# Token-order q reads and held output stores in a sliding-window attention + adapter-mixture kernel

## The chip, the cores and the metric

The kernel runs on one core of a Trainium2 chip. The metric is the device time of one execution, in microseconds. The engines are named as in the profile: PE (TensorE, with PEld for its weight loads), DVE (VectorE), ACT (ScalarE), POOL (GpSimd) and SP (SyncE, which here only issues DMAs; SPq is its queue).

## The reference, cut to what matters

Eight batches of eight heads, 576 tokens, head width 64. Each token attends to the tokens at most 32 away; the output of attention, with heads side by side (512 wide), goes through a mixture of eight rank-16 adapters of which the best two are used.

```
q, k, v: (8, 8, 576, 64) fp32
scores = q @ k^T / 8 ; scores = -1e9 where |i - j| > 32
attn   = softmax(scores) ; x = attn @ v            -> x: (4608, 512)
logits = x @ w_gate (512 x 8) ; top 2, softmax over the two -> w
out    = x + sum over the two e of w_e * (x @ A[e] (512 x 16)) @ B[e] (16 x 512)
```

## The kernel before

**Order.** A planner written in Python (`Planner.run`, L108) simulates the engines with estimated durations and due times and so fixes, before compilation, in which order each engine gets its instructions. `P.add(name, engine, duration, due, ...)` registers a task; `deps` are what it waits for, `soft` are dependences of order alone, `take` and `drop` reserve and free buffers of a pool. `LEAN` (L31) shifts the due time of each kind of task. On the chip each engine then runs its list strictly in order and waits on semaphores[...].

**Loads.** q and k come as tiles of 128 rows; a row holds 16 consecutive tokens of one head pair, so that `raw` is [128, 2, 16*64] in fp16 (POOL-issued DMA, `load`, L390). v comes in half batches through SP (`load_v`, L400) into one of 5 `vraw` buffers, and POOL casts it into `vbd` (`cast_v`, L451). The pool `ring` limits the v loads in flight. A batch has two v pairs (e = 0, 1) of two loads (h = 0, 1): 32 v loads in all.

**Scores.** PE transposes `raw` (L474), ACT moves k to `kT` in token order (L499) and DVE moves q to `qT`, [128, 16, 1156], where token 16 i + r lies at `qT[:, r, i]` (L497). A score tile (`score`, L539) covers four key blocks of 64 tokens for two head pairs: four matmuls put the mask into PSUM (L544), sixteen add k.q for 64 keys and 128 queries (L556). Its q operand is read as h, r, s (half, token within 16, group of 16), so the 128 query columns are in a permuted order, with four neighbouring elements at a time:

```
rhs=qT[p0:p0 + 64, :, c0:c0 + 8].rearrange("p r (h s) -> p h r s", h=2),
```

ACT takes exp into `PT` (L564). There are 36 score tiles.

**Attention output.** PE multiplies `PT` with `vbd` (`pv`, L595, and `pv_group` for the last batch, L624), DVE divides by the sum (`norm`, L613) into `xs`, rows in the permuted order.

**Adapters.** For each batch: transpose x (L700), DVE copies it (L705), logits and x @ A in one product (`zl`, L718), ACT copies (L731), gating on DVE (L740 to L761), transpose of the weighted z (L768), and its eviction by ACT (`moe_ez`, L771), which turns the columns to token order on the way. Then `moe_pd` (L782) adds z @ B and x; x is multiplied with `po_`, a permutation matrix made from the identity by POOL (L341), so that its rows come out in token order too. ACT moves the result to one of four `ob` tiles (L795), three blocks j for each batch, and SP stores it (`moe_st`, L797: L806 for single row groups, L801 for pairs), four store DMAs for each batch.

**Fillers.** `fill` (L319) places matmuls of a zero tile (L326) early in the kernel. `ldw` and `cw` load and cast the adapter weights through `Af`, `Gf` and `Bf`.

Of the kernel before, what the change touches and what calls it, by code (L numbers as in the profile page):

```python
# [23 lines left out]
class Planner:  # L24
# [5 lines left out]
    STICK = 0.3  # L30
    LEAN = {"cv": -0.54, "cvb": 46.78, "cw": -20.23, "cz": -10.49, "ek": 141.88,  # L31
            "eo": 48.48, "eoz": -5.02, "eq": -29.69, "ex": 32.88, "exx": -143.53,
            "exxz": -6.85, "ez": -111.14, "ezz": -35.61, "g1": 8.51, "g1z": 14.29,
            "g2": -11.82, "g2z": 45.73, "g3": 8.11, "g3z": -4.63, "ge": -13.97,
            "gez": -0.93, "ident": 11.01, "ld": -3.77, "ldw": 2.33, "lv": 89.29,
            "mask": -43.21, "nm": 2.69, "nmg": 12.33, "pad": 12.33, "pd": 138.17,
            "pdz": -1.64, "perm": 26.94, "pv": -35.98, "pvg": 4.54, "sc": 44.71,
            "st": -31.48, "stz": -8.25, "tr": -7.71, "wm": -4.16, "xT": -4.3, "xTz": -5.83,
            "zT": 88.34, "zTz": 6.27, "zero": 5.31, "zl": 45.91}
    SWITCH = 0.095  # L40
# [175 lines left out]
def kernel(  # L216
# [44 lines left out]

    NRAW, NKB, NVR, NVB, NPT, NX, NOB, NW = 3, 3, 5, 6, 6, 4, 4, 4
    HV = NP * NB // 2
# [18 lines left out]
    ident = const.tile([128, 128], F16, name="ident")  # L282
    po_ = const.tile([128, 128], F16, name="po_")
    mask = const.tile([128, 2, RR, 4], F16, name="mask")
    WA_sb = const.tile([128, NP, ER + E], F16, name="WA")
    B_sb = const.tile([128, DD], F16, name="Bsb")
    Af = const.tile([128, E, 4, R], F32, name="Af")
    Gf = const.tile([128, 4, E], F32, name="Gf")
    Bf = const.tile([128, DD], F32, name="Bf")

# [11 lines left out]
    P.pool("rc", 3)  # L302
    P.pool("ring", 3)
    place = {}
# [10 lines left out]

    zero = const.tile([128, DD], F16, name="zero")
    warm = []
# [22 lines left out]

    def c_perm():  # L341
        nc.gpsimd.tensor_copy(
            out=po_.rearrange("p (h s r) -> p h s r", h=2, s=4),
            in_=ident.rearrange("p (h r s) -> p h s r", h=2, s=4))

    def c_mask():
        nc.gpsimd.memset(mask, 0.0)
        for h in range(2):
            blk = mask[64 * h:64 * h + 64]
            nc.gpsimd.affine_select(out=blk, in_=blk, compare_op=ALU.is_ge, fill=NEG,  # L350
                                    base=0, channel_multiplier=-1,
                                    pattern=[[64, 2], [1, RR], [16, 4]])
            nc.gpsimd.affine_select(out=blk, in_=blk, compare_op=ALU.is_ge, fill=NEG,
                                    base=64, channel_multiplier=1,
                                    pattern=[[-64, 2], [-1, RR], [-16, 4]])

# [23 lines left out]
    P.add("ident", "POOL", 0.6, -19.9, c_ident, ["ld0.0.0"])  # L380
    P.add("perm", "POOL", 0.3, 0, c_perm, ["ident"])
    P.add("mask", "POOL", 2.3, -15, c_mask, ["ld0.0.1"])
# [17 lines left out]
    def load_v(b, e, h):  # L400
# [4 lines left out]
                          in_=src[:, HV * e:HV * e + HV])  # L405

    def load_w():
        nc.sync.dma_start(out=Af.rearrange("p e j r -> p e (j r)"),
                          in_=moe_A.rearrange("e (p j) r -> p e (j r)", j=4))
        nc.sync.dma_start(out=Gf.rearrange("p j e -> p (j e)"),  # L410
                          in_=moe_w_gate.rearrange("(p j) e -> p (j e)", j=4))
        nc.sync.dma_start(out=Bf, in_=moe_B.rearrange("e r d -> (e r) d"))

    def cast_w():
        nc.vector.tensor_copy(
            out=WA_sb[:, :, 0:ER].rearrange("p j (e r) -> p j e r", r=R),
            in_=Af.rearrange("p e j r -> p j e r"))
        nc.vector.tensor_copy(out=WA_sb[:, :, ER:], in_=Gf)
        nc.vector.tensor_copy(out=B_sb, in_=Bf)

    prev = []
    for t in range(NTI):
        hs = ((0, 64), (64, 128)) if t in SPLIT else ((0, 128),)
        for x, (lo, hi) in enumerate(hs):
            for w in (1, 0):
                due = tile_due(t) - 6 + 0.1 * (1 - w) if t else -20
                whole = lo == 0 and hi == 128 and 128 * t % BI + 128 > BI
                gate = GATE.get(t, []) if w == 1 and x == 0 else []
                P.add(f"ld{t}.{w}.{x}", "POOL", 1.2 if whole else 0.62, due + 0.3 * x,
                      lambda t=t, w=w, lo=lo, hi=hi: load(t, w, lo, hi),  # L430
                      prev + gate, lat=1.3,
                      take=[] if x else [("raw" + "qk"[w], t)])
                P.add(f"dq{t}.{w}.{x}", "Q0", 2.8 * (hi - lo) / 128, 0, None,
                      [f"ld{t}.{w}.{x}"], lat=0.8, pkt=172.0)
                prev = [f"ld{t}.{w}.{x}"]
    prev = ["pace"] if PACE else []
    for b in range(B):
        for e in range(2):
            for h in range(2):
# [5 lines left out]
                      pkt=18.0, drop=[("ring", (b, e, h))])  # L445
    P.add("ldw", "SP", 2.0, -2, load_w, WDEP, lat=1.2, take=[("ring", "w")])
    P.add("dw", "Q1", 1.8, -10, None, ["ldw"], lat=0.8, pkt=18.0, drop=[("ring", "w")])
    P.add("cw", "DVE", 1.8, 4, cast_w, ["dw"])

# [89 lines left out]
    def score(t):  # L539
        ps = W[wslot(("s", t))].rearrange("p (e i c) -> p e i c", e=2, c=128)  # L540
        for e in range(2):
            for hh in range(2):
                p0, o0 = 64 * hh, 64 * ((hh + e) % 2)
                nc.tensor.matmul(  # L544
                    out=ps[o0:o0 + 64, e], lhsT=ident[p0:p0 + 64, p0:p0 + 64],
                    rhs=bcast(mask[p0:p0 + 64].rearrange("p h r s -> p (h r s)"), 1, 4),
                    start=True, stop=False)
        for i in range(4):
            for e in range(2):
                u, a = seq(e, 4 * t + i)  # L550
                g = NB * u + a
                c0 = PADQ + 4 * g - 2
                c1 = 4 * (g % 32)
                for hh in range(2):
                    p0, o0 = 64 * hh, 64 * ((hh + e) % 2)
                    nc.tensor.matmul(  # L556
                        out=ps[o0:o0 + 64, e, i],
                        lhsT=kT[slot("kT", g // 32)][p0:p0 + 64, c1:c1 + 4].rearrange(
                            "p s r -> p (s r)"),
                        rhs=qT[p0:p0 + 64, :, c0:c0 + 8].rearrange("p r (h s) -> p h r s", h=2),  # L560
                        start=False, stop=(i == 3))
# [100 lines left out]
    for k_, (_, _, u) in enumerate(both):  # L662
# [4 lines left out]
        if isinstance(u, tuple):  # L667
            b, g = u
            if g == NG - 1:
# [6 lines left out]
                  drop=drop, soft=soft, mode="half", ni=12 if g in (0, NG - 1) else 16)  # L676
            P.add(f"nmg{b}.{g}", "DVE", 0.9, d + 1.0, lambda b=b, g=g: norm_group(b, g), [last_pv],
                  drop=[("W", ("p", u)), ("rc", u)])
            continue
        b, n = divmod(u, NP)  # L680
        if n % 2:
# [4 lines left out]
              soft=soft, mode="half", ni=18)  # L686
        P.add(f"nm{u}", "DVE", 1.4, k_ + 1.0, lambda u=u: norm(u), [f"pv{u}"],
              drop=[("W", ("p", u)), ("rc", u)])
# [82 lines left out]
    def moe_ez(b, k, g0, g1):  # L771
        tp = H16[slot("H", ("y", b, k))][:, 0:128 * (g1 - g0)]
        nc.scalar.copy(  # L773
            out=zTs[b % 2][:, g0:g1].rearrange("p g (h s r) -> p (g h) s r", h=2, s=4),
            in_=tp.rearrange("p (g r s) -> p g s r", r=RR, s=4))

# [5 lines left out]
    def moe_pd(b, j):  # L782
        pd = pdt(b, j)
        x = xs[slot("xs", b)]
        for i, g in enumerate(GG[j]):
            nc.tensor.matmul(out=pd[:, i], lhsT=zTs[b % 2][:, g], rhs=B_sb,  # L786
                             start=True, stop=False)
            nc.tensor.matmul(out=pd[:, i], lhsT=po_,  # L788
                             rhs=x[:, g],
# [18 lines left out]
    for b in range(B):  # L808
# [14 lines left out]
        for k_, (g0, g1) in enumerate(chunks):  # L823
# [7 lines left out]
            if not fine:  # L831
                P.add(f"cz{zn}", "ACT", 0.75, d0 - 1, lambda arg=arg: copy_z(*arg), [f"zl{b}.{k_}"]
                      + ([f"g3{b - 2}.{j}" for j in kold] if old else []), drop=[zb])
            P.add(f"g1{zn}", "DVE", 0.64 if n > 2 else 0.37, d0 - 1, lambda arg=arg: gate1(*arg),
                  [f"zl{b}.{k_}" if fine else f"cz{zn}"]
                  + ([f"zT{b - 2}.{j}" for j in kold] if old else []))
            P.add(f"ge{zn}", "ACT", 0.22, d0 - 1, lambda arg=arg: gate_e(*arg), [f"g1{zn}"])
            P.add(f"g2{zn}", "DVE", 1.57 if n > 2 else 1.1, d0 - 1, lambda arg=arg: gate2(*arg), [f"ge{zn}"])
            P.add(f"g3{zn}", "DVE", 0.35 + 0.15 * n, d0 - 1,
                  lambda arg=arg: gate3(*arg), [f"g2{zn}"], drop=[zb] if fine else [])  # L840
# [5 lines left out]
        for j in range(3):  # L846
            n = len(GG[j])
            k_ = j if fine else 0
            P.add(f"pd{z_}{b}.{j}", "PE", 0.43 * n, d0 + 1.2 + 0.7 * j, lambda b=b, j=j: moe_pd(b, j),
                  [f"ez{z_}{b}.{k_}", "perm"], soft=[f"pd{z_}{b}.{j - 1}"] if j else [],  # L850
                  take=[(PB[n], ("d", b, j)), ("ob", (b, j))], drop=[("xs", b)] if j == 2 else [],
# [4 lines left out]
            P.add(f"st{z_}{b}.{j}", "SP", 0.38 * (2 if j == 0 else 1), d0, lambda b=b, j=j: moe_st(b, j),  # L856
                  [f"eo{z_}{b}.{j}"], lat=1.2)
            P.add(f"ds{b}.{j}", "Q1", 0.7 * n, d0, None, [f"st{z_}{b}.{j}"],
# [42 lines left out]
```

## Time and profile before

| | |
|---|---|
| median of 3 runs | 143.47 us (143.44 to 145.68) |
| the profiled execution | 141.93 us |
| its span in the profile | 140.1 us |
| PE, DVE, ACT, POOL busy | 118.5, 94.2, 84.7, 64.0 us |
| DMA moved | 29.21 MB, mean 209 GB/s |

The durations in the profile come from the one profiled execution. A busy PE includes the latency of matmuls that overlap, so lengths of back-to-back groups, not the mean duration of one matmul, tell what PE spends. Each engine's idle time is put down to the semaphore that came last.

### The profile page before, as it was taken

To read this page: it belongs to the slowest core of one execution; us is meant where nothing else is said; L and a number is where in the kernel's file an instruction comes from. 1 tells how busy PE (TensorE), PEld (TensorE's weight loads), DVE (VectorE), ACT (ScalarE), POOL (GpSimd) and SP (SyncE) were. 2 spreads that over 40 slices of the span, in tenths; PEclk is the share of its full clock that TensorE was granted. 3 is DMA by queue.
4 is the path that set the end of the run, shared out by engine and by line. 5 is a ranking of instruction groups with operands and counts; after the bars stand their busy time and mean duration, and the time that the engine had idled before them with its cause. 6 is when DMAs were issued, how large, how long until landed. Compare 5 with 4: busy or idle time off the path is not lost.

```text
span 140.1 us, 5608 instructions
## 1 busy us (share of the span) xinstructions
PE 118.5 (85%) x2413; PEld 84.5 (60%) x2413; DVE 94.2 (67%) x288; ACT 84.7 (60%) x106; POOL 64.0 (46%) x78
## 2 busy tenths in 40 slices
PE   6779998969968489988999997999899989988430
PEld 2336573656947477576777784787585757854210
DVE  5773137074995993867879789699765996977500
ACT  3022471756535554787597769847977984387750
POOL 6876998003399973366019980193052630000000
PEclk9999999999999977999999999999999999999999
DMA  3999999999989999679999999999986944347864
GB/s 86 192 209 251 246 211 205 206 212 173 239 196 211 247 232 218 150 165 215 249 228 279 210 151 254 244 239 202 215 269 152 274 147 156 135 154 244 300 236 136
DMA packets 49000, 29.21 MB, mean 209 GB/s; under 512 B 39632, under 2 KB 39632, under 8 KB 48976
## 3 DMA queue, kind: packets, MB, share of 16 engines
q1 hardware_dynamic: 43824, 19.42, 53.6%
q0 software_dynamic: 5152, 9.44, 38.2%
q8 instruction: 19, 0.31, 0.9%
q14 instruction: 5, 0.04, 0.1%
HBM read 28.85 MB, written 9.44 MB: 273 GB/s over the span
## 4 chain that ended last, share of the span: by engine, by line
PE 51%; ACT 18%; DVE 17%; issue 5%; DMA 5%; ACTq 1%; POOL 1%; DVEq 0%; POOLq 0%
PE W L474 8%; ACT kT L499 7%; PE W L607 7%; PE W L718 6%; ACT PT L564 5%; PE W L326 5%; DMA raw<-in_q_dram 5%; PE W L544 4%; PE W L700 4%; PE W L786 4%; DVE xT L705 4%; PE W L556 3%; DVE xs L621 3%; PE W L788 3%; ACT ob L795 2%
## 5 line engine op out<-in xcount | busy, mean ns | idle before, releaser
L454 POOL TENSOR_SCALAR_AFFINE_SELECT vbd<-vraw 64x1152 f16<-64x1152 f32 x32 | 40.8, 1276 | 48.5 <-DMA vraw<-in_v_dram 45.1
L564 ACT ACTIVATE PT<-W 128x1024 f16<-128x1024 f32 x36 | 34.9, 1030 | 12.3 <-PE W L556 12.3
L621 DVE TENSOR_TENSOR xs<-W,rc 128x384 f16<-128x384 f32 (+1 forms) x56 | 27.5, 491 | 2.1 <-DVE rc L620 0.2
L795 ACT COPY ob<-W 128x1024 f32<-128x1024 f32 (+1 forms) x24 | 20.4, 873 | 6.4 <-PE W L788 2.5
L607 PE MATMUL W<-vbd,PT 128*64 128x130 f16 x504 | 19.2, 224 | 2.1 <-ACT PT L564 1.4
L499 ACT COPY kT<-W 128x1024 f16<-128x1024 f16 x16 | 15.6, 1016 | 8.5 <-PE W L474 7.7
L607 PEld LDWEIGHTS <-PT 128*64 128x64 f16 x504 | 16.0, 111 | 6.4 <-issue 3.8
L474 PE MATMUL W<-ident,raw 128*64 128x128 f16 x512 | 17.3, 220 | 2.6 <-DVE xT L705 2.3
L474 PEld LDWEIGHTS <-raw 128*64 128x64 f16 x512 | 15.1, 110 | 5.7 <-issue 5.1
L620 DVE RECIPROCAL rc<-W 128x6 f32<-128x6 f32 (+1 forms) x56 | 10.0, 179 | 10.7 <-PE W L607 10.6
L786 PE MATMUL W<-Bsb,zT 128*128 128x512 f16 x40 | 15.2, 380 | 2.2 <-ACT zT L773 0.8
L326 PE MATMUL W<-zero 128*128 128x512 f16 x37 | 14.3, 494 | 3.0 <-ACT kT L499 1.3
L544 PE MATMUL W<-mask,ident 64*64 64x512 f16 x144 | 15.8, 403 | 0.8 <-ACT PT L564 0.4
L556 PEld LDWEIGHTS <-kT 64*64 64x64 f16 x576 | 13.8, 110 | 3.8 <-issue 0.8
L556 PE MATMUL W<-qT,kT 64*64 64x128 f16 x576 | 16.0, 224 | 0.0
L497 DVE COPY qT<-W 128x1024 f16<-128x1024 f16 x16 | 10.4, 683 | 7.7 <-PE W L474 7.0
L705 DVE COPY xT<-W 128x1024 f16<-128x1024 f16 (+1 forms) x24 | 13.2, 593 | 3.4 <-PE W L700 2.3
L788 PE MATMUL W<-xs,po__112 128*128 128x512 f16 x40 | 15.1, 379 | 0.0
L718 PE MATMUL W<-WA,xT 128*128 128x136 f16 x160 | 12.3, 235 | 1.2 <-ACT PT L564 1.2
L718 PEld LDWEIGHTS <-xT 128*128 128x128 f16 x160 | 10.7, 104 | 2.9 <-issue 1.3
L700 PE MATMUL W<-ident,xs 128*128 128x128 f16 x160 | 10.7, 220 | 0.5 <-DVE xs L648 0.4
L397 POOL DMA_DIRECT2D raw<-in_k_dram x17 | 10.5, 620 | 0.8 <-POOLq L885 0.8
(51 smaller groups left out, 118.1 us busy)
## 6 DMA issues: line engine op xcount, KB each, us to landing
vraw<-in_v_dram SPq DMA_DIRECT2D x32, 288.0 KB, 8.0
out_dram<-ob SPq DMA_DIRECT2D x8, 512.0 KB, 3.8
out_dram<-ob SPq DMA_DIRECT2D x16, 192.0 KB, 3.0
out_dram<-ob SPq DMA_DIRECT2D x8, 256.0 KB, 2.9
raw<-in_k_dram POOLq DMA_DIRECT2D x4, 256.0 KB, 5.0
raw<-in_q_dram POOLq DMA_DIRECT2D x4, 256.0 KB, 7.4
raw<-in_k_dram POOLq DMA_DIRECT2D x2, 448.0 KB, 7.6
raw<-in_q_dram POOLq DMA_DIRECT2D x2, 448.0 KB, 8.3
```

The source lines that it names most:

```text
L326: nc.tensor.matmul(out=o, lhsT=zero[:, 0:128], rhs=zero, start=True, stop=True)
L454: nc.gpsimd.affine_select(out=vbt(b, e)[p, :, c:c + D], in_=vraw[slot("vr", (b, e))][p], compare_op=ALU.is_ge, fill=0.0, base=1, channel_m ...
L474: nc.tensor.matmul(out=tp[64 * hh:64 * hh + 64, 128 * (r % 8):128 * (r % 8) + 128], lhsT=src[:, hh, D * r:D * r + D], rhs=ident, is_transp ...
L499: nc.scalar.copy(out=kT[slot("kT", t)][:, :, 8 * h:8 * h + 8], in_=tp.rearrange("p r i -> p i r"))
L544: nc.tensor.matmul(out=ps[o0:o0 + 64, e], lhsT=ident[p0:p0 + 64, p0:p0 + 64], rhs=bcast(mask[p0:p0 + 64].rearrange("p h r s -> p (h r s)") ...
L556: nc.tensor.matmul(out=ps[o0:o0 + 64, e, i], lhsT=kT[slot("kT", g // 32)][p0:p0 + 64, c1:c1 + 4].rearrange("p s r -> p (s r)"), rhs=qT[p0: ...
L564: nc.scalar.activation(out=PTs[slot("PT", t)].rearrange("p e i c -> p (e i c)"), in_=W[wslot(("s", t))], func=AF.Exp, scale=1.0 / float(D) ...
L607: nc.tensor.matmul(out=po[o0:o0 + 64, GO[g]:GO[g] + 2 * VD], lhsT=PTs[slot("PT", s // 4)][:, e, s % 4, 64 * (1 - j):64 * (1 - j) + 64], rh ...
L621: nc.vector.tensor_tensor(out=x[:, g0:g1], in0=po[:, :, :, 0:D], in1=bcast(rc[:, g0:g1], 3, D), op=ALU.mult)
L718: nc.tensor.matmul(out=pz[:, g - g0, 0:ER + E], lhsT=xT[b % 2][:, g, c, :], rhs=WA_sb[:, c, :], start=(c == 0), stop=(c == NP - 1))
L786: nc.tensor.matmul(out=pd[:, i], lhsT=zTs[b % 2][:, g], rhs=B_sb, start=True, stop=False)
L795: nc.scalar.copy(out=obs[slot("ob", (b, j))][:, 0:n], in_=pd[:, 0:n])
```

## The change

The q operand of the score matmuls is read as s, r (group of 16, then token within it), which is token order; the mask tile is laid out in the same order. So the columns of `PT` and the rows of `xs` are in token order, `moe_ez` is a plain copy, and `moe_pd` multiplies x with the identity; `po_` is gone. The stores of a batch b get a dependence of order on the last v load of batch b + 6 (for b = 0 and 1). The output tiles become 7 in place of 4, and the ring of v loads 5 in place of 3. The adapter weights are staged in one of the output tiles, the zeros of the fillers in an `xs` buffer. Loads of q and k depend on one another by order alone. All entries of `LEAN` and some planned durations of DVE tasks have new values.

```diff
-    LEAN = {"cv": -0.54, "cvb": 46.78, "cw": -20.23, "cz": -10.49, "ek": 141.88,
...
+    LEAN = {"cv": 238.6, "cvb": 171.14, "cw": -69.72, "cz": 82.21, "ek": 8.02, "eo": 383.9,
...
-    NRAW, NKB, NVR, NVB, NPT, NX, NOB, NW = 3, 3, 5, 6, 6, 4, 4, 4
+    NRAW, NKB, NVR, NVB, NPT, NX, NOB, NW = 3, 3, 5, 6, 6, 4, 7, 4
+    HOLD = 6
...
-    po_ = const.tile([128, 128], F16, name="po_")
-    mask = const.tile([128, 2, RR, 4], F16, name="mask")
+    mask = const.tile([128, 2, 4, RR], F16, name="mask")
...
-    Af = const.tile([128, E, 4, R], F32, name="Af")
-    Bf = const.tile([128, DD], F32, name="Bf")
...
-    P.pool("ring", 3)
+    P.pool("ring", 5)
...
-    zero = const.tile([128, DD], F16, name="zero")
+    zero = xs[NX - 1][:, 0]
...
-    def c_perm():
-        nc.gpsimd.tensor_copy(
-            out=po_.rearrange("p (h s r) -> p h s r", h=2, s=4),
-            in_=ident.rearrange("p (h r s) -> p h s r", h=2, s=4))
...
-                                    pattern=[[64, 2], [1, RR], [16, 4]])
+                                    pattern=[[64, 2], [16, 4], [1, RR]])
...
+    def stage_w():
+        w = obs[slot("ob", "w")]
+        return w[:, 0].rearrange("p (e j r) -> p e j r", e=E, j=4), w[:, 1]
...
-                      prev + gate, lat=1.3,
+                      gate, lat=1.3, soft=prev,
...
-    P.add("ldw", "SP", 2.0, -2, load_w, WDEP, lat=1.2, take=[("ring", "w")])
+    P.add("ldw", "SP", 2.0, -2, load_w, WDEP, lat=1.2, take=[("ring", "w"), ("ob", "w")])
...
-                        rhs=qT[p0:p0 + 64, :, c0:c0 + 8].rearrange("p r (h s) -> p h r s", h=2),
+                        rhs=qT[p0:p0 + 64, :, c0:c0 + 8].rearrange("p r s -> p s r"),
...
-            out=zTs[b % 2][:, g0:g1].rearrange("p g (h s r) -> p (g h) s r", h=2, s=4),
-            in_=tp.rearrange("p (g r s) -> p g s r", r=RR, s=4))
+            out=zTs[b % 2][:, g0:g1].rearrange("p g t -> p (g t)"), in_=tp)
...
-            nc.tensor.matmul(out=pd[:, i], lhsT=po_,
+            nc.tensor.matmul(out=pd[:, i], lhsT=ident,
...
-                  [f"eo{z_}{b}.{j}"], lat=1.2)
+                  [f"eo{z_}{b}.{j}"], lat=1.2,
+                  soft=[f"lv{b + HOLD}.1.1"] if b + HOLD < B else [])
```

## The prediction

> **What bounds the kernel now.** I first read the engine totals and the slices of the page. PE is busy for 85% of the span and near full from the second slice on; the DMA row stands at 9 until about slice 30, dips once at slices 16 and 17 (56 to 63 us), and falls after that.
>
> ```profile
> PE 118.5 (85%) x2413; PEld 84.5 (60%) x2413; DVE 94.2 (67%) x288; ACT 84.7 (60%) x106; POOL 64.0 (46%) x78
> DMA  3999999999989999679999999999986944347864
> ```
>
> Busy PE is not yet streaming PE, so the stages come next: one row for each 10 us, engines in the order PE, PEld, DVE, ACT, POOL, then clock, DMA share and GB/s.
>
> ```profile
> 40.00:50.00 10.00, 6.45 (x177) 5.40 (x173) 8.07 (x23) 4.62 (x6) 9.71 (x11) 1.00 1.07 214
> ...
> 60.00:70.00 10.00, 9.09 (x205) 7.19 (x199) 8.09 (x23) 6.88 (x9) 4.06 (x6) 1.00 0.99 202
> 70.00:80.00 10.00, 9.49 (x238) 7.45 (x239) 7.97 (x23) 8.05 (x11) 6.62 (x7) 1.00 1.04 244
> 80.00:90.00 10.00, 9.05 (x229) 6.84 (x225) 8.49 (x27) 7.87 (x10) 3.63 (x4) 1.00 1.05 210
> 90.00:100.00 10.00, 9.77 (x235) 8.21 (x235) 8.35 (x24) 7.00 (x9) 5.14 (x5) 1.00 1.02 220
> 100.00:110.00 10.00, 9.27 (x205) 6.59 (x207) 6.95 (x24) 8.15 (x12) 4.20 (x4) 1.00 0.85 223
> 110.00:120.00 10.00, 9.38 (x183) 7.30 (x175) 8.59 (x23) 7.07 (x9) 2.15 (x2) 1.00 0.61 196
> 120.00:130.00 10.00, 9.15 (x92) 5.30 (x89) 8.39 (x39) 6.96 (x13) 0.00 (x0) 1.00 0.49 163
> ```
>
> From 60 to 130 us PE is busy 65.2 of 70 us, so 4.8 us is all the idle that a better supply could return there. The other hole is 40 to 50 us (3.55 us idle), before any store. The loads are just as full until 110 us. PE sets the pace and DMA is close behind it: work added to PE shows, and DMA taken away returns at most PE's idle time.
>
> Then what a score tile costs PE, from the chain that ended last (start, length, what): four mask matmuls of 512 columns, then sixteen q.k matmuls of 128 columns (some records are missing), three tiles back to back.
>
> ```profile
> 96.80 0.24 PE W L556 x13
> 97.04 0.22 PE W L544 x4
> 97.25 0.24 PE W L556 x14
> 97.50 0.25 PE W L544 x4
> 97.74 0.24 PE W L556 x13
> ```
>
> Four mask matmuls take 0.22 us, the time of 512 columns, so four 64x64 tiles of the array stream at once and a column takes 0.43 ns. Sixteen matmuls of 128 columns are four rounds, again 512 columns and 0.22 us; measured 0.24. The q read streams at full rate now.
>
> Last, the SP queue, in order of time, and what POOL's casts of v wait for.
>
> ```profile
> 33.73 16.52 SPq L404 DMA_DIRECT2D vraw<-in_v_dram  x9
> 57.87 0.84 SPq L806 DMA_DIRECT2D out_dram<-ob  x2
> 58.80 1.58 SPq L404 DMA_DIRECT2D vraw<-in_v_dram  x1
> ...
> SPq L404 <- POOL vbd L454: 17.4, 11, 4.0
> ...
> POOL vbd L454 <- DMA vraw<-in_v_dram: 45.1, 13, 9.2
> ```
>
> Between 50.25 and 57.87 SP issues nothing: batch 0's store stands next and waits for the eviction of its block on ACT, and the v loads wait behind it. That is the DMA dip at 56 to 63 us. POOL waits 45.1 us for v; PE hardly notices.
>
> **What the Trainium skill says.** "SBUF — State Buffer", section Door 1 (the note on cachelines), says that SBUF has 16-byte lines, that at least two accesses to a line are needed for full bandwidth, and that each access to a new line pays. This bears on the new q read: one column per line. Before, the read takes four neighbouring halves (8 bytes) and then jumps, and L556 shows that this costs nothing; the trace shows no one-per-line read by PE. "TensorEngine Tiling (Array Packing)", Key Properties, has tiles work in parallel; the 0.22 us above agrees. "DMA: Bandwidth & Descriptors", Queues, rings and completion order, has each DMA engine take turns between the queues, so a store and a load on SP's own queue go one behind the other, which the SP rows fit.
>
> **Part by part.**
>
> *The strided q read (L560).* Inner order changes from s to r, a jump of 1156 halves (2312 bytes) at each column. Same 576 instructions, same columns. Bounds: nothing, if the line change is hidden. At the other end, four columns to a line now run at full rate, so a line change takes at most four column times if it is not overlapped: 128 changes x 1.7 ns = 218 ns where 55 stood, four rounds 0.87 for 0.22 us, +0.65 us a tile, x36 = +23.4 us. I take half rate, the plain reading of "two hits needed": +0.22 us a tile, +7.9 us of PE in all. Counts of L544 by stage put 24 tiles behind 50 us and 12 before. Behind 50 us PE is above 90% busy and nothing hides it: 24 x 0.22 = +5.3. Before that PE has the 3.55 us hole and the filler matmuls (L326, 29 of them from 10 to 40 us); I charge half of 12 x 0.22 = +1.3. Sum **+6.6 us**.
>
> *Mask, z and output without permutation.* The four affine_selects of the mask keep their shape (528 and 522 ns). The copy that makes po_ goes: 290 ns on POOL at 3.87 us, ahead of the fourth load, not on the first q load that starts PE: 0 (cover gone: -0.3). The z eviction L773 becomes contiguous: now 697 ns for 640 columns, against 1016 for 1024 at L499, which reads with jumps too, and 727 for 680 at L731, which reads without; all about 1 ns a column, so 0. The identity as weights in place of po_: same load (98 ns), 0.
>
> *Stores of batches 0 and 1 held.* Four stores a batch, eight of 32, with 0.4 us of SP issue each, go behind v loads that now stand after them. Batch 0's wait for the last v load of batch 6 (the 28th), batch 1's for the 32nd. This frees SP at 50 us and takes 2 x 1.18 MB out of the loading phase: at 226 GB/s with a 0.66 share (130 to 140 us), 342 GB/s, that is 6.9 us of DMA. They land in the stretch behind 100 us, where the share is 0.85 to 0.49. The last v cast, at 112.8 us now, comes earlier; but what it can give back is PE's 4.8 us of idle, part of which is engine hand-over. I take half: **-2.4** (ends 0 and -4.8).
>
> *Buffers.* Seven output tiles for four, of which the weights borrow one until they are cast (same DMAs, same casts of 417 and 419 ns); a deeper v ring (5 for 3) keeps SP's queue filled. The zeros of the fillers move into xs3, which batch 3 fills after the last filler (before 40 us). 0 each.
>
> *New priorities.* Every engine's order is planned anew. The hole at 47.2 to 49.6 us, where PE waits for DVE's L705, cost 2.3 us and a clock share of 0.72 from 50 to 56 us, 1.7 us more: some 4 us that a different order may lose or make twice. I take **-0.6**, ends +3 and -4.
>
> Sum: 6.6 - 2.4 - 0.6 = +3.6 us on the profiled execution of 141.93 us (span 140.1 and 1.8 around it): 145.5. The profiled one lies 1.5 us under the median of the runs, 143.47, so the forecast is **147.1 us**.
>
> **Rivals.**
>
> *The strided read is free (faster).* For it: the two column halves of the array already read the same 64 partitions at once at full rate, so the read has some reserve; the transposes of x load weights with 8-byte jumps at 114 ns against 104 without. Against: those are still two hits a line. PE's work then stays as it is, and the order and the loads decide: -2.4 - 0.6, up to -4.8 - 4. Centre -3.6: 139.9 us. It decides from a price below 0.08 us a tile (3.0 us / 36).
>
> *The line change costs four columns, or the two streams of a partition take turns.* +0.65 a tile: 24 x 0.65 + 12 x 0.65 x 0.6 = +20, less 3: 160 us. Nothing in the profile excludes it; the skill's words speak for the smaller price.
>
> *The held stores starve the output tiles.* Batches 0 and 1 take six of the seven; the second block of batch 2 then needs batch 0's first store landed, hence the 28th v load issued. Now that block runs at about 87 us and the 28th load is issued at about 93. Without the stores in its way it needs 11 loads of 288 KB and one q and k tile at 209 GB/s, some 18 us from 50: 70 us. So 15 us of margin, unless casts come late for want of vbd buffers. If it does, PE stands in order: +3 on top of the forecast, 150 us.
>
> **How the numbers follow.** Half rate 0.45, free 0.36, four columns 0.09, starved 0.10. Two per cent (2.9 us), about what a measurement of this kernel can tell from no change, puts the bounds at 140.6 and 146.3. Half rate, 143.5 to 151: slower 0.29, same 0.14, faster 0.02. Free, 136 to 143: faster 0.25, same 0.10, slower 0.01. The other two: slower 0.18, same 0.01. So faster 0.27, same 0.25, slower 0.48. The range runs from 138.5 (most of the free case) to 151.5 (half rate all exposed and nothing returned); the four-column case is left out.
>
> **What would show it.** L556 spaced at about 0.44 us a tile between mask groups, against 0.24: right; at 0.24: the free rival; at 0.9: the third case. SP should issue v loads without a store between 50 us and the 28th, the dip at 56 to 63 us should go, and the last v cast should end before 105 us. L773 at 697 ns again. If PE waits for a block's eviction with stores outstanding near batch 2's pd, the output tiles starve. Wrong altogether: L556 at 0.24 and a longer time, which only the new order could cause.

## The result, and the profile after

The changed kernel takes 163.04 us (median of 4 runs, 161.93 to 165.14) against 143.45 us before: a ratio of 1.138, 95% interval 1.124 to 1.151. Some executions of a kernel are slower than its others: medians here count all of them, ratios and their intervals only the faster ones of both kernels. The forecast was 147.1 us in a range of 138.5 to 151.5, so the way was right and the size was not; the rival "the line change costs four columns" had 160 us. The profiled execution took 163.31 us, 161.6 us of it in the span.

First the page of the changed kernel: the engine totals, the DMA slices, and the group of the score matmuls (line L554 now; busy us, mean ns of one, idle before).

```profile
PE 140.2 (87%) x2413; PEld 89.2 (55%) x2413; DVE 94.4 (58%) x288; ACT 87.0 (54%) x106; POOL 63.3 (39%) x77
DMA  4999999999998999999999999720323044019993
...
L554 PE MATMUL W<-qT,kT 64*64 64x128 f16 x576 | 40.9, 415 | 0.0
```

PE has 21.7 us more of busy time with the same 2413 matmuls; the 576 score matmuls alone go from 16.0 to 40.9 us. DVE, ACT and POOL have about what they had. The DMA dip in the middle is gone and the loads end earlier, and no gain from that shows in the time.

The chain that ended last, over three score tiles (start, length, what), answers to the rows of 96.80 us before:

```profile
64.37 0.22 PE W L542 x4
64.59 0.97 PE W L554 x15
65.56 0.22 PE W L542 x4
65.78 0.96 PE W L554 x14
66.74 0.22 PE W L542 x3
```

The mask groups still take 0.22 us. The score group takes 0.96 where it took 0.24: +0.72 us a tile, 26 us in 36 tiles.

The late stages (PE, PEld, DVE, ACT, POOL, then clock, DMA share, GB/s):

```profile
110.00:120.00 10.00, 9.69 (x182) 6.31 (x172) 7.09 (x25) 6.91 (x7) 0.00 (x0) 1.00 0.14 48
120.00:130.00 10.00, 10.00 (x190) 6.12 (x185) 5.20 (x20) 7.04 (x9) 0.00 (x0) 1.00 0.22 75
130.00:140.00 10.00, 10.00 (x155) 6.52 (x155) 6.36 (x16) 5.88 (x7) 0.00 (x0) 1.00 0.35 121
```

PE is busy for 97 to 100% while POOL has nothing left and the DMA share is 0.14 to 0.35: in these stages PE sets the pace. The SP queue in order of time (start, length, what):

```profile
28.74 54.60 SPq L396 DMA_DIRECT2D vraw<-in_v_dram  x20
83.43 1.54 SPq L803 DMA_DIRECT2D out_dram<-ob  x2
...
89.44 9.67 SPq L396 DMA_DIRECT2D vraw<-in_v_dram  x4
```

And the last row of POOL's timeline:

```profile
99.20 5.72 POOL L452 TENSOR_SCALAR_AFFINE_SELECT vbd<-vraw 64x1152 f16<-64x1152 f32 x4 [9.22 <-DMA vraw<-in_v_dram]
```

Twenty v loads run in one stretch with no store among them, the 28th ends at 83.34 us, and the first store stands right behind it, as the hold asks. The last v cast ends at 104.9 us, 9 us earlier than before (114.0), in a kernel that is 21 us longer.

### The profile page after: what moved, and what is told of

Read it like the earlier page. It is cut to its first block, busy times and chain, and to the rows that moved or that the text cites. A ratio compares the mean times of both kernels' runs of the same rounds, so it can differ in the third digit from the quotient of the medians.

```text
span 161.6 us, 5603 instructions
## 1 busy us (share of the span) xinstructions
PE 140.2 (87%) x2413; PEld 89.2 (55%) x2413; DVE 94.4 (58%) x288; ACT 87.0 (54%) x106; POOL 63.3 (39%) x77
## 4 chain that ended last, share of the span: by engine, by line
PE 60%; DVE 23%; DMA 4%; issue 4%; ACT 4%; ACTq 1%; POOL 0%; DVEq 0%; POOLq 0%
PE W L554 20%; DVE xs L619 8%; PE W L542 7%; PE W L605 5%; PE W L324 5%; PE W L716 5%; DMA raw<-in_q_dram 4%; PE W L472 4%; PE W L783 3%; PE W L698 3%; PE W L785 3%; DVE zs L759 3%; DVE rc L618 3%; DVE xT L703 2%; DVE qT L495 2%
## 5 line engine op out<-in xcount | busy, mean ns | idle before, releaser
L562 ACT ACTIVATE PT<-W 128x1024 f16<-128x1024 f32 x36 | 36.9, 1024 | 32.4 <-PE W L554 29.8
L554 PE MATMUL W<-qT,kT 64*64 64x128 f16 x576 | 40.9, 415 | 0.0
L554 PEld LDWEIGHTS <-kT 64*64 64x64 f16 x576 | 19.2, 121 | 12.0 <-issue 0.5
L605 PE MATMUL W<-vbd,PT 128*64 128x130 f16 x504 | 17.3, 221 | 1.0 <-DVE xs L619 0.8
L605 PEld LDWEIGHTS <-PT 128*64 128x64 f16 x504 | 15.1, 110 | 5.5 <-issue 3.2
L324 PE MATMUL W<-xs 128*128 128x512 f16 x37 | 13.9, 474 | 2.9 <-DVE qT L495 1.7
L785 PE MATMUL W<-xs,ident 128*128 128x512 f16 x40 | 15.2, 379 | 0.0
L716 PE MATMUL W<-WA,xT 128*128 128x136 f16 x160 | 11.2, 223 | 1.0 <-DVE WA L416 1.0
L716 PEld LDWEIGHTS <-xT 128*128 128x128 f16 x160 | 9.7, 98 | 4.2 <-issue 3.3
L698 PEld LDWEIGHTS <-xs 128*128 128x128 f16 x160 | 9.7, 114 | 2.3 <-issue 1.1
```

The lines of the kernel that those rows point to most:

```text
L324: nc.tensor.matmul(out=o, lhsT=zero[:, 0:128], rhs=zero, start=True, stop=True)
L554: nc.tensor.matmul(out=ps[o0:o0 + 64, e, i], lhsT=kT[slot("kT", g // 32)][p0:p0 + 64, c1:c1 + 4].rearrange("p s r -> p (s r)"), rhs=qT[p0: ...
L562: nc.scalar.activation(out=PTs[slot("PT", t)].rearrange("p e i c -> p (e i c)"), in_=W[wslot(("s", t))], func=AF.Exp, scale=1.0 / float(D) ...
L605: nc.tensor.matmul(out=po[o0:o0 + 64, GO[g]:GO[g] + 2 * VD], lhsT=PTs[slot("PT", s // 4)][:, e, s % 4, 64 * (1 - j):64 * (1 - j) + 64], rh ...
L698: nc.tensor.matmul(out=tp[:, o:o + 128], lhsT=x[:, g].rearrange("p (k c) -> p c k", c=4)[:, c], rhs=ident, is_transpose=True, start=True, ...
L716: nc.tensor.matmul(out=pz[:, g - g0, 0:ER + E], lhsT=xT[b % 2][:, g, c, :], rhs=WA_sb[:, c, :], start=(c == 0), stop=(c == NP - 1))
```

## The experiments

Each ratio is against the kernel before on the same chip.

**1. What a column costs by how it is read.** Extra matmuls with q as moving operand (the `rhs` of a matmul) stand behind the last block of the kernel before; they lengthen it (251 us) and leave the output alone.

```diff
+        flat = qT.rearrange("p r w -> p (r w)")
...
+        NM = 12
...
+        for _ in range(NM):
+            nc.tensor.matmul(out=o0, lhsT=ident, rhs=flat[:, 0:512], start=True, stop=True)
...
```

The same follows with runs of 8, 4, 2 and 1 neighbours, with steps of 2, 4, 8 and 16 elements, and then with 64x64 tiles: four at a time (runs of 4, of 1), pairs, one alone.

> The kernel before with extra matmuls behind its last block (they add to the time; the output is untouched): groups of twelve 512-column matmuls of the full array with the same weights, the moving operand read from q in runs of 512, 8, 4, 2 and 1 neighbouring elements, then with steps of 2, 4, 8 and 16 elements; then 64x64 tiles four at a time (runs of 4 and of 1), two tiles on different partitions, two tiles on the same partitions, and one tile alone. Theory A (each stream pays about 1.7 ns for every column that comes from a new line, tiles independent): full array 0.22 us a matmul for runs of 512, 8 and 4, 0.44 for runs of 2, 0.87 for runs of 1; one tile, two tiles on different partitions, two on the same and four at a time all 0.87 us per round. Theory B (half rate for one column a line, and the two streams of the same partitions take turns): full array 0.44 for runs of 1 and 0.22 for runs of 2; one tile or two on different partitions 0.44, two on the same partitions and four at a time 0.87. Theory C (full rate, but tiles no longer run side by side): full array 0.22 in every form, four tiles 0.87 per round, two tiles 0.44, one 0.22. Steps: if only the line counts, step 2 and 4 elements (4 and 2 hits a line) are as in runs of 4 and 2, step 8 and 16 as runs of 1.

The chain over the full-array groups of that kernel, in the order of the text: 512 neighbours, runs of 8, 4, 2, 1, steps of 2, 4, 8, 16; twelve matmuls of 512 columns in each.

```profile
136.19 2.59 PE W L876 x12
138.78 2.72 PE W L878 x12
141.50 2.87 PE W L880 x12
144.37 5.68 PE W L882 x12
150.05 11.44 PE W L884 x12
161.49 4.05 PE W L886 x12
165.54 5.43 PE W L888 x12
170.97 10.80 PE W L890 x12
181.77 11.01 PE W L892 x12
```

Divided by twelve: 0.216, 0.227, 0.239, 0.473, 0.953 us for runs of 512, 8, 4, 2 and 1. Take a line as 16 bytes, eight of q's 16-bit elements. From runs of 4 down the time follows the number of moves to another line: 128, 256 and 512 of them at 1.87, 1.85 and 1.86 ns. Above that the columns set it, 0.42 ns each. The steps agree to within some 5%: 8 and 16 elements, one column a line, take 0.900 and 0.918; step 4, two a line, takes 0.452 (1.76 to 1.79 ns a line); step 2, four a line, took 0.226 in its last matmuls (its first took 0.427, under a halved clock, of which below). So it is not the jump from column to column that costs, since step 2 jumps at every column too. And a line that was read before costs again: the runs of 1 return to some 70 lines (16 stretches of 64 bytes) all the time and pay no less than step 8, in which every column has a line of its own. "SBUF — State Buffer" (the Trainium skill, section Door 1) gives lines of 16 bytes, and they fit; its two hits a line for full bandwidth do not hold for PE here. Two hits give half the rate (0.473 us), four come within 11% of the full one (0.239 against 0.216).

The tiles, from the starts of the rounds in the trace:

| 64x64 tiles at a time, 512 columns | us a round |
|---|---|
| four, runs of 4 | 0.240 |
| four, runs of 1 | 0.953 |
| two on different partitions, runs of 1 | 0.953 |
| two on the same partitions, runs of 1 | 0.953 |
| two on the same partitions, runs of 2 | 0.473 |
| one alone, runs of 1 | 0.953 |

How many tiles share the array or the partitions makes no difference in these forms. That is Theory A; B (streams take turns) and C (tiles lose their concurrency) are out. It also shows where the kernel before stood: its runs of 4 were at 128 lines x 1.86 ns = 0.238 us a round, on the edge at which lines begin to cost more than columns. There was nothing to spare.

**2, 3 and 4. The two halves of the change apart.** Run 2 keeps everything but the token order:

```diff
-                        rhs=qT[p0:p0 + 64, :, c0:c0 + 8].rearrange("p r s -> p s r"),
+                        rhs=qT[p0:p0 + 64, :, c0:c0 + 8].rearrange("p r (h s) -> p h r s", h=2),
```

(with the mask, the z eviction and `po_` to match).

> The changed kernel with the q read, the mask, the z eviction and the permutation matrix as they were before; held stores, buffers and the new order stay. If the strided read is the whole loss, this is at or below the time before: 143.4 less the 2.4 to 4.8 us of idle that the loads can return, 138 to 142 us. If the new order or the held stores cost time of their own, it stays above 146 us.

146.23 us, ratio 1.023 (1.015 to 1.032). Run 3 puts the token order alone into the kernel before.

> The kernel before with the strided q read alone (mask, z eviction and identity to match), old order and stores. A score tile rises from 0.24 to 0.96 us as in the changed kernel: 24 tiles after 50 us at 0.72 and 12 before at half of it make 21.6 us, 165 us. If the old order hides less than the new one did, more, up to 143.4 + 26 = 169; if it is under 160, the rest of the change costs time.

159.31 us, ratio 1.116 (1.111 to 1.122). Two tiles of it from the chain:

```profile
63.02 0.96 PE W L556 x16
63.98 0.22 PE W L544 x4
64.20 0.96 PE W L556 x16
```

Run 4 is run 2 without the hold.

```diff
-                  soft=[f"lv{b + HOLD}.1.1"] if b + HOLD < B else [])
+                  soft=[])
```

> As the second kernel (q read as before, rest of the change kept), but the stores of batches 0 and 1 wait for no v load; buffers, ring and priorities as in the change. If the hold is what frees the loads, this is 2 to 5 us slower than the second kernel. If the order and buffers do it, within 1 us of it.

147.61 us, ratio 1.032 (1.023 to 1.040). The strided read costs 16.2 us by itself, the rest 3.1 us, and together they make the 19.6 us of the change. By the medians of runs 2 and 4 the hold is worth 1.4 us within the new order; the two intervals overlap, so not even that is certain.

**5 and 6. Order and buffers crossed.** Run 5 is run 2 with the old `LEAN` and the old planned durations; run 6 is the kernel before with the new ones.

```diff
-            P.add(f"g2{zn}", "DVE", 1.57 if n > 2 else 1.1, d0 - 1, lambda arg=arg: gate2(*arg), [f"ge{zn}"])
+            P.add(f"g2{zn}", "DVE", 1.0 if n > 2 else 0.88, d0 - 1, lambda arg=arg: gate2(*arg), [f"ge{zn}"])
```

(run 6, with all entries of `LEAN` and the other four durations).

> The second kernel (q read as before, stores held, seven output tiles, ring of five, weights staged) with the priorities and the planned durations of before. If the new priorities cost the 3 us, this comes back to 143 us or, with the loads freed, to 139 to 142. If held stores and buffers cost them, it stays at 146.

> The kernel before with the priorities and planned durations of the change, nothing else. If the priorities cost the 3 us, 146 us or more; if they are neutral and the buffers cost it, 143.

149.77 us (145.46 to 152.24, too wide for a ratio) and 148.07 us, ratio 1.034 (1.023 to 1.045). The new order on the old buffers is slower than before by its interval; the old order on the new buffers is slower by its median against 143.33 us, with a wide scatter. Neither is shown to be better than buffers and order of the change together. So the 3 us cannot be given to one of the two. That an order suits only the buffers for which it was laid out would explain it, but runs 10 and 13 below, with an order searched for these buffers, are no faster; the cause of the 3 us stays open.

**7. The half-rate case on purpose.** q is read in runs of two in the kernel before, mask, z eviction and `po_` to match.

```diff
-                        rhs=qT[p0:p0 + 64, :, c0:c0 + 8].rearrange("p r (h s) -> p h r s", h=2),
+                        rhs=qT[p0:p0 + 64, :, c0:c0 + 8].rearrange("p r (s u) -> p s r u", u=2),
```

> The kernel before with q read in runs of two neighbouring elements (mask, z eviction and permutation matrix to match). By the forms measured at the end of the kernel a round of 512 columns takes 0.47 us, so this is the half-rate case of the prediction: +0.23 us a tile, 36 tiles 8.3 us. The prediction put 6.6 of 7.9 us on the span; the strided read alone put 16.1 of 26 (62%) there, which would make 5.1 of 8.3. Expected 148 to 150 us; under 146 the share that shows is not the same for small costs.

```profile
56.98 0.48 PE W L556 x14
57.47 0.22 PE W L544 x4
57.69 0.48 PE W L556 x12
```

A score group takes 0.48 us, as the lines say (256 x 1.86 ns), and the kernel 147.18 us, ratio 1.019 (1.007 to 1.032): 2.8 us for 8.6 us of added PE work, a third of it, where the prediction let 6.6 of 7.9 show. The interval (0.9 to 4.6 us) excludes that share. The runs scatter, though (144.68 to 150.47 us), and the medians lie 3.9 us apart, 45%: how much shows is less certain than that it is less than the prediction's share.

**8. Token order without a strided read on PE.** DVE stores q with the 16 tokens of a group side by side.

```diff
-                nc.vector.tensor_copy(out=qT[:, 8 * h:8 * h + 8, c0:c0 + 128], in_=tp)
+                nc.vector.tensor_copy(out=qT[:, c0:c0 + 128, 8 * h:8 * h + 8],
+                                      in_=tp.rearrange("p r i -> p i r"))
```

(with the tile `qT`, its zero columns, the second copy and the q read to match, and mask, z eviction and identity as in the change).

> The kernel before, but DVE stores q in token order (16 neighbouring elements a token), so that the score matmuls read 128 neighbouring columns in token order; mask, z eviction and identity as in the change. PE saves at most 0.24 - 0.216 us a tile, 0.9 us in all. The DVE copies (683 ns now) read PSUM with jumps: if they slow to the 1016 ns that ACT takes for the same, 16 of them add 5.3 us to DVE, which is busy for 67%; 143 to 146 us. If DVE's copy keeps its time, 142 to 143.

A score group in the chain of that kernel, and then DVE's copy of q in its groups:

```profile
98.90 0.22 PE W L557 x16
```

```profile
L497 DVE COPY qT<-W 128x1024 f16<-128x1024 f16 x16 | 18.8, 1214 | 5.7 <-PE W L474 5.7
```

PE gets its 0.22 us, and the copy goes from 683 to 1214 ns, more than the 1016 that I took from ACT: 8.5 us more of DVE in these sixteen. 146.75 us, ratio 1.028 (1.022 to 1.034). Token order had a price in both places where q was turned; of the three ways tried, the permutation matrix of before, a 290 ns copy once and a weight load that is needed anyway, is the cheapest.

**9. The planned DVE durations.** In the waits of run 2 PE stands for the gated z:

```profile
PE W L773 <- DVE zs L766: 3.9, 4, 2.7
```

(waiter and releaser, us in total, times, longest.) Run 9 is run 2 with the five old durations.

```diff
-            P.add(f"g2{zn}", "DVE", 1.0 if n > 2 else 0.88, d0 - 1, lambda arg=arg: gate2(*arg), [f"ge{zn}"])
+            P.add(f"g2{zn}", "DVE", 1.57 if n > 2 else 1.1, d0 - 1, lambda arg=arg: gate2(*arg), [f"ge{zn}"])
```

> The second kernel (rest of the change, q read as before) with the new priorities but the planned durations of before for normalization and gating on DVE (gating part two 1.57 us, not 1.0; the profile before has 1.44 for it). In the second kernel PE waits 3.9 us for the gated z (1.3 at most before). If the shortened durations are what costs the 3 us, this returns to 143 to 144 us and that wait falls under 2 us. If the priorities or the buffers cost it, it stays at 146 or more.

```profile
PE W L773 <- DVE zs L766: 2.4, 1, 2.4
```

145.84 us against 145.03 on that chip, ratio 1.012 (1.005 to 1.019). The wait shrinks to one occurrence of 2.4 us and about half of the loss goes, but this too moves the whole order, and the interval touches that of run 2. I take it as support, not as proof.

**10 to 13. Orders planned anew.** Runs 10 and 13 keep the rest of the change with the old durations and search `LEAN` again; runs 11 and 12 keep the whole change, strided read included, with the price of a score tile corrected, the old durations and `LEAN` searched again.

```diff
-        P.add(f"sc{t}", "PE", 0.47, TB * t / NB, lambda t=t: score(t),
+        P.add(f"sc{t}", "PE", 1.19, TB * t / NB, lambda t=t: score(t),
```

> As the ninth, with priorities searched anew for these buffers and durations, so that the order fits the held stores. If held stores and the deeper ring are worth the 2.4 us that the prediction gave them, 141 us or less; if the loads were hidden already and only the fit of the order counts, 142 to 145, no better than before.

> The changed kernel, strided read included, with a score tile planned at 1.19 us in place of 0.47 (what the trace shows), the old DVE durations, and priorities searched anew. If the loss is bare PE work, at most a few us come back: 158 to 163. If the order laid out for cheap score tiles made half of it, 152 to 155.

148.45 us, ratio 1.031 (1.022 to 1.039), and 159.89 us, ratio 1.110 (1.100 to 1.121). Both orders made the identity late. The wait in run 11:

```profile
PE W L478 <- POOL ident masks.py:199: 8.0, 1, 8.0
```

Its first score tile came at 17.6 us, that of run 10 at 18.2. Runs 12 and 13 keep the start of the change (first tile at 14.7 and 14.9 us).

> As the eleventh (strided read, score tile planned at 1.19 us, priorities searched anew), but with the start of the change kept, so that the identity is made after the fifth load; in the eleventh PE waited 8.0 us for it and the first score tile came at 17.6 us, not 14.9. If that start cost its 2.7 us, 157 us; if PE work is the bound, the start is absorbed later and it stays at 160.

> As the tenth (held stores and buffers, q read as before, old planned durations, priorities searched anew), with the start of the change kept; in the tenth the first score tile came at 18.2 us, not 14.4 to 14.8, which can hide up to 3.5 us of gain. If the held stores are worth the 2.4 us of the prediction, 141 to 143 us; if they are worth nothing, 145 to 147.

156.26 us and 147.85 us, against 144.96 us of the kernel before on that chip (140.1 to 147.2; too wide for a ratio). Against the change (1.138) run 11 is better, with intervals that do not overlap: some 4 us of the 19.6 went with that order and the short durations. That is not shown to come from the known price of a score tile: run 3, whose order was laid out for the old price, has 1.116, and its interval overlaps that of run 11. Run 12 is at 1.08 by the medians but at 1.10 by the lowest runs (154.34 against 140.08), so it shows no more than run 11. By the medians run 11 is still 14.9 us above the kernel before. No order tried with the held stores was faster than the kernel before, and no version here beats it.

## Why the prediction was right or wrong

*What bounds the kernel*: right. PE set the pace, and the added PE work is what lengthened it.

*The strided q read*: this is the term that failed. The place, the 36 tiles and the mechanism held; the price was +0.22 us a tile and measured +0.72. The step that failed is the choice "I take half rate, the plain reading of 'two hits needed'". The prediction's own bound, four columns' time for a line (+0.65), was the better number, and it came from the trace: four columns to a line ran at nearly full rate. It treated that as the far end, gave it 9 chances in 100 and left it out of the range; run 1 shows that it was the edge (0.240 us against 0.216 for neighbours). The profile had a hint of it: a score group took 0.24 us and a mask group with as many columns 0.22, and I passed that over as full rate. It was the line price already: with neighbours in place of runs of 4 the group takes 0.22 (run 8). Worked out with the 0.24 us instead, the bound is 0.24 / 128 = 1.88 ns a line and 0.96 us for 512 lines, +0.72 us a tile, as measured.

*How much of it shows*: 83% was charged (6.6 of 7.9). Run 3 shows 16.2 of 26 us, 62%; run 7 shows 2.8 of 8.6, 33%. A share taken from busy tenths was too high for both. Where the rest went is not shown: PE's idle time is 21.6 us in the profile before (140.1 - 118.5) and 19.0 in that of run 3 (157.9 - 138.9), so filled gaps account for 2.6 of the 9.8 us at most, and the rest lies in time that the profile counts as busy. With the right price the prediction's share would have made 24 x 0.72 + 12 x 0.36 = 21.6 us for the read, 5.4 more than run 3 has.

*Mask, z and output without permutation*: right where seen. The z eviction takes 699 ns against 697, the identity's weight load 98 as before.

*The held stores*: the mechanism came as told (no store before the 28th load, the dip gone, the last cast before 105 us), with one size off: the 28th load was issued by 83.3 us, not 70. The gain of 2.4 us did not come. It was bounded by PE's idle time, but that idle was not waiting for v. PE's longest waits before (us in total, times, longest), and the first one that names a load:

```profile
PE W L474 <- DVE xT L705: 2.3, 1, 2.3
PE W L607 <- ACT PT L564: 1.4, 4, 0.7
...
PE W L488 <- DMA raw<-in_q_dram: 0.8, 1, 0.8
```

None names POOL's cast of v. Freeing a supplier for which PE does not wait returned 1.4 us by the medians of runs 2 and 4, which is not certain.

*New priorities*: the sign was wrong, and the ends given (+3 and -4) did not hold it: order and buffers without the hold cost 4.5 us (run 4), the order and its durations alone on the old buffers 4.7 (run 6), each by the medians. With the hold the rest of the change costs 2.3%, where -3.0 us was the sum forecast for hold and order. What the order does differently can be seen: the first adapter product of batch 0 starts at 70.4 us in run 2, against 55.8 before (80.1 in the changed kernel). Whether the later outputs heaped up at the end are what costs the 3 us was not isolated.

*Starved output tiles*: not seen. No eviction in the changed kernel waits for a store, though the 28th load was later than I reckoned.

The two errors of opposite sign on the read (price too low, share too high) and the missed sign of the rest make the difference: 16.2 (run 3) and 3.1 (run 2) make 19.3, against the 19.6 measured and the 3.6 forecast. That the rival's 160 us came so near is in part luck: it had the price nearly right, but it charged +20 for the read, where run 3 has 16.2, and took 3 off for the rest, where run 2 adds 3.1, and the two cancel.

## What to carry to other kernels

Price a matmul's moving operand by lines as well as by columns: here the larger of columns x 0.42 ns and moves to another line x 1.8 to 1.9 ns, with one, two or four tiles at work, so four 16-bit neighbours in a line were nearly free (0.24 us for 512 columns against 0.216) and two cost double (0.473). When the trace gives only a bound (this many to a line run at full rate), take the bound as the likely price until something shows reserve. And ask of a freed transfer whether the engine that sets the pace ever waited for it.

## What the runs showed of the hardware

The 1.86 ns for a line do not depend on the granted clock of PE. Four stretches of run 1 with 64x64 tiles: four at a time with runs of 4 (the first two rows) and with runs of 1, then two on the same partitions with runs of 1 (PE and PEld busy with their counts, clock, DMA share, GB/s):

```profile
193.20:194.90 1.70, 1.70 (x24) 0.69 (x20) 0.50 0.00 0
195.20:196.50 1.30, 1.30 (x28) 0.64 (x24) 1.00 0.00 0
197.60:207.00 9.40, 9.40 (x44) 1.29 (x40) 1.00 0.00 0
...
217.00:227.00 10.00, 10.00 (x25) 1.53 (x21) 0.50 0.00 0
```

With runs of 1 the rounds take 0.953 us in both stretches, at the full clock and at the half. Reads that cost nothing by lines do run slower at the half: the tiles with runs of 4 took 0.427 us a round until the clock came back, then 0.240, and the group with step 2 took 0.427 us a matmul, then 0.226.

PE is busy throughout, and the clock is halved all the same. In this one execution it fell three times (at 154.0, 174.5 and 212.0 us), each time within matmuls that read one column a line, and came back twice (at 164.2 and 194.9 us), each time within 3 us of the start of a group with four columns a line. Whether it is the slow reading that brings the clock down was not tried apart.

The clock is not what made the change slow. From 20 to 150 us the stages of the changed kernel show the full clock. From 10 to 20 us it has 0.60, but run 2, without the strided read, has 0.59 there; and the four runs of run 3, with a mean clock of 0.963 to 0.989, lie within 0.9 us of each other.
